# Nine unread matmuls at the start of an attention and expert kernel, and transfers priced by kind in its list schedule

## The chip, the core and the metric

The kernel runs on one core of a Trainium2 chip. The core's engines each work through a queue of their own, in order: TensorE (PE; its weight loads are shown as PEld), VectorE (DVE), ScalarE (ACT), GpSimd (POOL) and SyncE (SP), which here issues nearly all transfers. The metric is the device time of one execution in microseconds, as the median of several runs.

## What is computed

Two batches, eight heads, 768 positions and 64 numbers per head. Attention is masked by a hash: a query sees the keys in the same one of 64 buckets, and the bucket is the signs of six projections. The result goes through two expert stages of dense products, the first with a plain product of two branches, the second with a sigmoid gate.

```python
q_bits = (np.einsum('bhsd,dk->bhsk', q, proj) > 0)      # the same for k
mask = q_bucket[:, :, :, None] == k_bucket[:, :, None, :]
scores = np.where(mask, scale * np.matmul(q, k.transpose(0, 1, 3, 2)), -1000000000.0)
attn = np.exp(scores - max); attn = attn / (sum + 1e-09); x = np.matmul(attn, v)
...
h = ((x @ w1) * (x @ w2)) @ w3;  x = h @ w_out           # 512 -> 1024 -> 1024 -> 512
val = x @ w_val; y = (sigmoid(x @ w_gate) * val) @ w_out # 512 -> 1536 -> 512
```

q, k, v and proj are float32, the weights arrive as 64-bit floats and are decoded on the chip.

## The kernel before

**Precision and tiles.** A float32 operand is split into a high and a low part (both fp32r), and a product is three passes: high by high, high by low, low by high. That is why there are pairs of names: aq and bq, ak and bk, wth and wtl, pt_0 and pt_1.

**Attention, 16 heads.** Per head h, `prep` scales the queries on POOL (L495), casts them to aq (L496), makes the difference bq (L497), each in two halves, and copies parts of them by transfers (L500, L501). The hash of a half is three matmuls with the projection pq (L479) into a bank gps, a sign on ACT (sg, L481), a matmul with a pattern pat (L482) and a comparison on DVE (ft, L504), whose result is moved next to the operands by further transfers (L508 to L510). So the mask is part of the score product itself. `first_head` does the same for head 0 with the work spread over ACT, DVE and POOL (L533 to L546). Per tile g of 128 queries (six per head): scores s (four matmuls, L558 and L561), their maximum sm on DVE (L567), the exponential e with its row sum on ACT (L577), transposes tp on PE (L612), their split into pt_0 on ACT (L615) and pt_1 on DVE (L617), and twelve matmuls av with the split values spv (L630; the split is L466 and L467), for two tiles at a time. Every head's row sums go through `emit_rows`: a sum on POOL (L588), a reciprocal rs, a transfer to a row in DRAM (L591) and a broadcast back into rr (L595). `emit_scale` multiplies the output of a pair of heads in xall by rr on POOL (L602), for t in steps of 2 of 6 chunks, so three instructions of 128x256 per pair; the result is read by the first expert stage only.

**Filler.** Between the tiles the weights come in: `stage_next` issues a load st of 512 KB (L412), and `decode` turns it into float32 with two instructions on ACT (da L428, dr L429), two on POOL (dr L430, da L431) and two on DVE (L432, L437). The product of the last two matrices of the first stage (wacc, L685, from wo and t, split at L673 and L680) and the first part of that stage (L794) run in the same gaps.

**Expert stages.** From about 340 us on it is nearly all `three` (L794), with splits on ACT, POOL and DVE.

**What sets the order.** `order_engines` takes all instructions with their dependencies, buffers and a priority, and runs a list schedule in a model of the chip: `cost` gives each instruction a duration, `step` a delay between engines, a transfer lands by a formula from a single rate, and PE has a clock with two levels. Then 6,000 random changes of priorities are tried, and each that does not lengthen the modelled whole is kept. The order found is imposed on each engine. So a change of one price anywhere in the model can change the order everywhere.

## Time and profile before

| | us |
|---|---|
| three timed runs | 766.24, 766.40, 767.06 |
| median | 766.4 |
| the profiled execution | 769.23 |
| its span, first to last instruction | 767.4 |
| PE busy | 746.2 |
| DVE, ACT, POOL busy | 626.3, 525.3, 431.4 |

The profiled execution's own time is 1.8 us above its span, and 2.8 us above the median. Busy is the time in which an engine works on an instruction, waits left out; matmuls overlap, so a busy PE may still be paced by something. The chain that ended last is made of PE for 81% of the span, of ACT for 7%, DVE 5%, POOL 4%, waits for issue 2% and transfers 2%. Windows are stretches of time counted from the first instruction; the granted clock is the share of TensorE's full clock in a stretch.

### The profile page before, as it was taken

How to read it: one execution, taken by the hardware profiler on the slowest of the kernel's cores; microseconds unless marked ns; L12 is line 12 of the kernel's file. 1: busy time of each engine (PE TensorE's matmuls, PEld its weight loads, DVE VectorE, ACT ScalarE, POOL GpSimd, SP SyncE). 2: the span in 40 equal slices, each digit the busy share in tenths (PEclk: the TensorE clock that was granted, in tenths of full speed). 3: DMA queues.
4: the chain of work that ended last, by engine and by line, in shares of the span. 5: the costliest groups of instructions: out<-in, count | busy, mean ns of one | idle time of the engine just before them, and what ended most of it. 6: DMA issues, size and time to landing. Idle time of an engine off the chain costs nothing.

```text
span 767.4 us, 11480 instructions
## 1 busy us (share of the span) xinstructions
PE 746.2 (97%) x3896; PEld 638.3 (83%) x3896; DVE 626.3 (82%) x970; ACT 525.3 (68%) x986; POOL 431.4 (56%) x475
## 2 busy tenths in 40 slices
PE   5898999999999999999999999999999999999997
PEld 4787889888989889988888888888888888888886
DVE  6996988776899789869999998788789787676743
ACT  7897988877899889777555568865746444442353
POOL 7767787865577574446655544797654433442000
PEclk9999999999999999999999999999999999999999
DMA  9975767533457755200111143432100000000011
GB/s 289 231 175 149 193 175 205 140 100 115 151 148 168 176 141 142 87 12 1 54 40 45 56 164 124 151 125 97 55 0 28 28 1 1 1 0 2 1 55 56
DMA packets 28506, 74.46 MB, mean 97 GB/s; under 512 B 6048, under 2 KB 8352, under 8 KB 28448
## 3 DMA queue, kind: packets, MB, share of 16 engines
q1 hardware_dynamic: 28368, 73.73, 33.1%
q8 instruction: 31, 0.51, 0.3%
q14 instruction: 27, 0.22, 0.1%
q10 hardware_dynamic: 80, 0.00, 0.0%
HBM read 52.82 MB, written 3.19 MB: 73 GB/s over the span
## 4 chain that ended last, share of the span: by engine, by line
PE 81%; ACT 7%; DVE 5%; POOL 4%; issue 2%; DMA 2%; SPq 0%; DVEq 0%; ACTq 0%; POOLq 0%
PE pa L794 18%; PE pb L794 15%; PE m L794 11%; PE av L630 6%; PE wacc L685 5%; PE tp L612 5%; PE p L794 4%; PE npa L794 4%; PE npb L794 4%; PE s L558 3%; PE s L561 3%; ACT e L577 2%; PE y L794 2%; ACT pt L615 2%; PE gps L479 2%
## 5 line engine op out<-in xcount | busy, mean ns | idle before, releaser
L617 DVE TENSOR_TENSOR pt<-tp,pt 128x512 fp32r<-128x512 f32 x144 | 95.0, 683 | 9.0 <-ACT pt L615 8.1
L612 PE MATMUL tp<-idf,e 128*128 128x128 f32 x576 | 100.3, 276 | 1.8 <-DVE xall L643 0.8
L567 DVE TENSOR_REDUCE sm<-s 128x1 f32<-128x768 f32 x96 | 90.2, 948 | 11.3 <-PE s L561 11.0
L577 ACT ACTIVATE e<-s,sm 128x768 f32<-128x768 f32 x96 | 86.9, 906 | 8.1 <-DVE sm L567 7.6
L431 POOL TENSOR_SCALAR da<-da 128x512 f32<-128x512 f32 x76 | 52.4, 689 | 66.1 <-ACT da L428 59.0
L615 ACT ACTIVATE pt<-tp 128x512 fp32r<-128x512 f32 x144 | 82.4, 599 | 8.6 <-PE tp L612 7.2
L612 PEld LDWEIGHTS tp<-idf,e 128*128 128x128 f32 x576 | 72.0, 141 | 11.6 <-DVE xall L643 2.0
L630 PE MATMUL av<-pt,spv 128*128 128x256 f32 x576 | 79.2, 286 | 0.7 <-DVE ft L504 0.3
L630 PEld LDWEIGHTS av<-pt,spv 128*128 128x128 f32 x576 | 73.2, 190 | 3.6 <-DVE pt L617 1.8
L430 POOL TENSOR_SCALAR dr<-st 128x512 bf16<-128x512 f32 x76 | 67.3, 887 | 6.9 <-issue 1.1
L558 PE MATMUL s<-bk,bq 128*128 128x384 f32 x192 | 62.2, 377 | 6.1 <-ACT e L577 5.4
L561 PE MATMUL s<-ak,aq 128*128 128x384 f32 x192 | 60.8, 376 | 0.0
L429 ACT ACTIVATE dr<-st 128x512 int16<-128x512 uint32 x76 | 60.1, 791 | 0.0
L685 PE MATMUL wacc<-wo,t 128*128 128x512 f32 x192 | 59.3, 407 | 0.0
L428 ACT ACTIVATE da<-st 128x512 f32<-128x512 f32 x76 | 51.1, 672 | 12.0 <-DVE xall L437 3.7
L432 DVE TENSOR_SCALAR da<-da 128x512 uint32<-128x512 uint32 x76 | 47.3, 625 | 9.8 <-POOL da L431 9.8
L558 PEld LDWEIGHTS s<-bk,bq 128*128 128x128 f32 x192 | 36.0, 195 | 11.8 <-ACT e L577 7.8
L794 PE MATMUL pa<-xsx,swh 128*128 128x512 f32 x136 | 42.5, 390 | 0.2 <-DVE w2r L957 0.2
L920 POOL TENSOR_TENSOR swl<-w2r,swh 128x512 fp32r<-128x512 f32 x16 | 21.0, 1313 | 31.2 <-ACT swh L367 28.9
L561 PEld LDWEIGHTS s<-ak,aq 128*128 128x128 f32 x192 | 36.6, 195 | 1.8 <-DVE ak L544 0.3
L685 PEld LDWEIGHTS wacc<-wo,t 128*128 128x128 f32 x192 | 34.3, 189 | 4.2 <-ACT t L367 0.2
L794 PE MATMUL m<-wtl,gh 128*128 128x512 f32 x96 | 37.2, 389 | 0.0
(338 smaller groups left out, 2187.3 us busy)
## 6 DMA issues: line engine op xcount, KB each, us to landing
st<-in_moe_w_dram SPq DMA_DIRECT2D x32, 512.0 KB, 5.2
st<-in_moe_w_out_dram SPq DMA_DIRECT2D x20, 512.0 KB, 3.3
st<-in_moe_w_gate_dram SPq DMA_DIRECT2D x12, 512.0 KB, 3.3
st<-in_moe_w_val_dram SPq DMA_DIRECT2D x12, 512.0 KB, 3.2
qk<-in_qk_dram SPq DMA_DIRECT2D x15, 384.0 KB, 4.3
rawv<-in_v_dram SPq DMA_DIRECT2D x16, 192.0 KB, 2.4
rr<-row SPq DMA_DIRECT2D x16, 192.0 KB, 5.0
out_dram<-o SPq DMA_DIRECT2D x12, 256.0 KB, 2.0
```

Source lines behind the costliest of these rows:

```text
L429: act.activation(out=r.bitcast(I16)[:, 0::2], in_=lw, func=AF.Copy, scale=2.0 ** -29)
L430: pool.tensor_scalar(out=r.bitcast(BF16)[:, 1::2], in0=f(hw), scalar1=0.0, scalar2=1.0, op0=ALU.mult, op1=ALU.mult)
L558: pe.matmul(s[:, half, :HS], lhsT=m["bq"][:, qs], rhs=m["bk"][:, ks], start=True, stop=False)
L561: pe.matmul(s[:, half, :HS], lhsT=m["aq"][:, qs], rhs=m["ak"][:, ks], start=False, stop=True)
L567: dve.tensor_reduce(out=b, in_=s[:, :, :HS], op=ALU.max, axis=AX.XY, negate=True)
L577: act.activation(out=e.rearrange("p (a c) -> p a c", a=2), in_=s[:, :, :HS], func=AF.Exp, bias=sm, scale=1.0, accum_out=su_t[h][:, t:t + 1],)
L612: pe.transpose(ps[:, i * P:(i + 1) * P], e_t[g - g % 2 + a][:, c * P:(c + 1) * P], idf)
L615: act.activation(out=dh, in_=src, func=AF.Copy)
L617: dve.tensor_tensor(out=d, in0=src, in1=f(dh), op=ALU.subtract)
L630: pe.matmul(acc[:w.shape[1], :2 * P].rearrange("p (a t) -> p a t", a=2), lhsT=w, rhs=r[:, :, c], start=(c == 0 and i == 0), stop=(c == NT ...
L685: pe.matmul(acc, lhsT=t3[x][:, j], rhs=wo[y][:, j], start=(j == 0 and n == 0), stop=(j == NF1 - 1 and n == 2))
L794: mm = pe.matmul(ps, lhsT=lhs[x], rhs=rhs[y], start=start and n == 0, stop=stop and n == 2)
```

## The change

There are two parts. On the chip, DVE sets a 128x128 piece of xall to zero first, and PE multiplies it by itself five times into a bank named ramp; after each half of head 0's cast and difference PE multiplies them by the projection once more into the same bank, with a priority 150 lower, so that the list schedule places these four where it likes. Nobody reads the bank. The scaling of a pair is written as two instructions of 128x384 in place of three of 128x256. In the model, ACT's price for 256 columns of a bank falls from 405 to 290 ns and DVE's price per column of a small two-operand instruction on a bank from 1.17 to 1.0; a transfer has a delay of 1.7 us in place of 2.9, a rate by kind (250 bytes per ns for 64-bit weights, 205 for what is read from a tile, 340 for the rest, in place of 300 for all) and at least 0.3 us, and lands 3.0 us later where it reads a row in DRAM and 1.0 us later otherwise, in place of 0.9.

```diff
--- before.py
+++ after.py
@@ -95,7 +95,7 @@
             return n / 2.4 * passes + (14 if n == 512 else 16 if passes == 1 else 2 if passes == 2 else 4)
         if e == "Activation":
             if banks:
-                return {768: 878, 512: 478, 256: 405}.get(n, 470)
+                return {768: 878, 512: 478, 256: 290}.get(n, 470)
             return 40 + n + (96 if es == 2 else 0)
         if e == "Pool":
             port[k] = True
@@ -110,7 +110,7 @@
             if two and n >= 512:
                 return 600
             if two:
-                return 85 + n * 1.17 if banks else 60 + n * 1.1
+                return 85 + n * 1.0 if banks else 60 + n * 1.1
             return 589 if banks else 60 + n * 0.55
         return 500
 
@@ -171,6 +171,10 @@
     costs = [cost(k) for k in range(N)]
     left0 = [len(deps[k]) + len(starts[k]) for k in range(N)]
     loads = [type(i).__name__.startswith("InstDMA") for i in ins]
+    wide = [mybir.dt.size(i.outs[0].dtype) == 8 for i in ins]
+    local = [[r[0] for r in map(region, i.ins) if r] for i in ins]
+    rate = [250 if wide[k] else 205 if local[k] else 340 for k in range(N)]
+    slack = [3000 if any(t.startswith("row") for t in local[k]) else 1000 for k in range(N)]
 
     HORIZON, STRIDE = 30000.0, 15000.0
 
@@ -281,8 +285,8 @@
                         free[e] = done = begin + c
                         if loads[k]:
                             n = count(ins[k].outs[0]) * list(ins[k].outs[0].ap)[0][1] * mybir.dt.size(ins[k].outs[0].dtype)
-                            dma = max(now + 2900, dma) + n / 300
-                            done = dma + 900
+                            dma = max(now + 1700, dma) + max(300, n / rate[k])
+                            done = dma + slack[k]
                         tick += 2
                         heapq.heappush(events, (done, tick - 1, "end", k))
                         heapq.heappush(events, (free[e], tick, "free", k))
@@ -518,7 +522,12 @@
         m = mats[0]
         t = [ap_.tile([P, S], F32, tag="e", name=f"qk0{i}", bufs=4) for i in range(2)]
         act.dma_start(out=pq_raw, in_=proj)
+        x = xall[:, 0, 0:P]
+        dve.memset(x, 0.0)
         dve.memset(zb, -2.0 ** -64)
+        ps = psT.tile([P, 512], F32, tag="t", name="ramp")
+        for _ in range(5):
+            pe.matmul(ps[:, :P], lhsT=x, rhs=x, start=True, stop=True)
         act.activation(out=warm, in_=zb, func=AF.Exp)
         for half in range(2):
             hs = slice(half * HS, (half + 1) * HS)
@@ -533,6 +542,10 @@
             act.activation(out=m["aq"][:, hs], in_=t[0][:, hs], func=AF.Copy, scale=scl[:, 0:1])
             dve.scalar_tensor_tensor(out=m["bq"][:, hs], in0=t[0][:, hs], scalar=scl[:, 0:1], in1=f(m["aq"][:, hs]),
                                      op0=ALU.mult, op1=ALU.subtract)
+            tc.cur_priority += 150
+            for x in ("aq", "bq"):
+                pe.matmul(ps[:, :HS], lhsT=pq[0], rhs=m[x][:, hs], start=True, stop=True)
+            tc.cur_priority -= 150
         load_qk(2)
         act_copy(m["bk"][0:D], t[1][0:D])
         dve.tensor_copy(m["bk"][D:P], f(m["bq"][D:P]))
@@ -598,8 +611,8 @@
         b, hh = divmod(h, H)
         x = xall[:, hh // 2, b * S:(b + 1) * S].rearrange("p (c q) -> p c q", c=NT)
         r = rr_t.pop(h // 2).rearrange("p (q c) -> p c q", c=NT)
-        for t in range(0, NT, 2):
-            pool.tensor_tensor(out=x[:, t:t + 2], in0=x[:, t:t + 2], in1=r[:, t:t + 2], op=ALU.mult)
+        for t in range(0, NT, NT // 2):
+            pool.tensor_tensor(out=x[:, t:t + NT // 2], in0=x[:, t:t + NT // 2], in1=r[:, t:t + NT // 2], op=ALU.mult)
 
     def emit_T(g, j):
 
```

The numbers move the order of the whole program. In the next listings a number behind a name is the buffer's, and the lines L of the changed kernel are 4 larger in the decoder, in `prep` and its helpers and 13 larger from `first_head`'s second half on. The first place is POOL around the preparation of head 4 (aq4, bq4) and the scaling of heads 0 and 1 (xall by rr0). Before:

```order
L431 TENSOR_SCALAR da_948<-da_948 128x512
L495 TENSOR_SCALAR qk5_628<-qk5_628 64x384 x2
L430 TENSOR_SCALAR dr_949<-st_705 128x512
L466 CAST spv3_903<-rawv3_532 128x6x64
L467 TENSOR_TENSOR spv3_903<-rawv3_532,spv3_903 128x6x64
L602 TENSOR_TENSOR xall_79<-xall_79,rr0_306 128x256 x3
L496 CAST aq4_776<-qk4_381 128x384
L497 TENSOR_TENSOR bq4_777<-qk4_381,aq4_776 128x384
L496 CAST aq4_776<-qk4_381 128x384
L497 TENSOR_TENSOR bq4_777<-qk4_381,aq4_776 128x384
L588 TENSOR_SCALAR su2_612<-su2_612 128x6
L680 TENSOR_TENSOR wo1_93<-wor3_443,wo0_92 128x512
```

The same place on POOL in the changed kernel:

```order
L693 TENSOR_TENSOR wo1_93<-wor3_454,wo0_92 128x512
L435 TENSOR_SCALAR da_990<-da_990 128x512
L470 CAST spv3_913<-rawv3_543 128x6x64
L471 TENSOR_TENSOR spv3_913<-rawv3_543,spv3_913 128x6x64
L434 TENSOR_SCALAR dr_991<-st_800 128x512
L500 CAST aq4_786<-qk4_392 128x384
L501 TENSOR_TENSOR bq4_787<-qk4_392,aq4_786 128x384
L500 CAST aq4_786<-qk4_392 128x384
L501 TENSOR_TENSOR bq4_787<-qk4_392,aq4_786 128x384
L615 TENSOR_TENSOR xall_79<-xall_79,rr0_317 128x384 x2
L693 TENSOR_TENSOR wo1_93<-wor4_455,wo0_92 128x512
L601 TENSOR_SCALAR su2_623<-su2_623 128x6
```

The scaling went from ahead of head 4's casts to behind them; one wo, one da and one dr came ahead of them. The second place is DVE at the start (pq the projection, pat the pattern made from bits, bq0, bk0 and ak0 operands of head 0, spv0 its split values, sm the maximum). Before:

```order
L1107 TENSOR_TENSOR bits_117<-bits_117 64x128
L1108 TENSOR_SCALAR bits_117<-bits_117 64x128
L1111 TENSOR_SCALAR pat_72<-bits_117 32x64 x2
L1114 CAST pq0_70<-pq_raw_73 64x6 x2
L1115 TENSOR_TENSOR pq1_71<-pq_raw_73,pq0_70 64x6 x2
L534 SCALAR_TENSOR_TENSOR bq0_96<-qk00_100,scl_75,aq0_95 128x384 x2
L538 CAST bk0_98<-bq0_96 64x768
L544 TENSOR_SCALAR ak0_97<-gps_148,thr_74 64x384
L466 CAST spv0_242<-rawv0_111 128x6x64
L544 TENSOR_SCALAR ak0_97<-gps_155,thr_74 64x384
L567 TENSOR_REDUCE sm0_184<-s0_84 128x1
```

DVE at the start of the changed kernel:

```order
L1120 TENSOR_TENSOR bits_124<-bits_124 64x128
L1127 CAST pq0_70<-pq_raw_73 64x6
L1121 TENSOR_SCALAR bits_124<-bits_124 64x128
L1127 CAST pq0_70<-pq_raw_73 64x6
L1128 TENSOR_TENSOR pq1_71<-pq_raw_73,pq0_70 64x6 x2
L1124 TENSOR_SCALAR pat_72<-bits_124 32x64 x2
L543 SCALAR_TENSOR_TENSOR bq0_96<-qk00_100,scl_75,aq0_95 128x384 x2
L551 CAST bk0_98<-bq0_96 64x768
L470 CAST spv0_253<-rawv0_118 128x6x64
L557 TENSOR_SCALAR ak0_97<-gps_159,thr_74 64x384
L557 TENSOR_SCALAR ak0_97<-gps_166,thr_74 64x384
L580 TENSOR_REDUCE sm0_195<-s0_84 128x1
```

The mask of bits and pat went behind the first cast of the projection, which waits for a transfer, and the cast of the values, which waits for another, went ahead of both comparisons ak0. The third place is ACT behind those comparisons, where the first weights are decoded (da, dr) and the first exponentials (e) run. Before:

```order
L546 ACTIVATE aq0_95<-gps_155,nthr_76 64x384
L428 ACTIVATE da_456<-st_448 128x512
L577 ACTIVATE e0_187,su0_186<-s0_84,sm0_184 128x768
L577 ACTIVATE e1_195,su0_186<-s1_85,sm1_193 128x768
L429 ACTIVATE dr_457<-st_448 128x512
L428 ACTIVATE da_466<-st_450 128x512
L481 ACTIVATE sg_225<-gps_221,zb_78 128x384
L429 ACTIVATE dr_467<-st_450 128x512
```

ACT at the same place in the changed kernel:

```order
L559 ACTIVATE aq0_95<-gps_166,nthr_76 64x384
L432 ACTIVATE da_467<-st_459 128x512
L433 ACTIVATE dr_468<-st_459 128x512
L590 ACTIVATE e0_198,su0_197<-s0_84,sm0_195 128x768
L432 ACTIVATE da_477<-st_461 128x512
L590 ACTIVATE e1_206,su0_197<-s1_85,sm1_204 128x768
L433 ACTIVATE dr_478<-st_461 128x512
L485 ACTIVATE sg_236<-gps_232,zb_78 128x384
```

The first weight's dr went ahead of the first exponential, and the second's da ahead of the second.

## Rows read from the trace of the kernel before

**Rows 1.** Page, part 1: busy us, share of the span, instructions, of each engine

```profile
PE 746.2 (97%) x3896; PEld 638.3 (83%) x3896; DVE 626.3 (82%) x970; ACT 525.3 (68%) x986; POOL 431.4 (56%) x475
```

**Rows 2.** Windows of 20 us: busy time by engine, columns as in the first line

```profile
core 0: us, PE busy (x) PEld busy (x) DVE busy (x) ACT busy (x) POOL busy (x), PEclk, DMA share, GB/s
40.00:60.00 20.00, 18.64 (x129) 16.64 (x127) 19.65 (x31) 19.78 (x42) 12.95 (x18) 1.00 0.67 162
60.00:80.00 20.00, 17.44 (x108) 16.15 (x108) 14.17 (x24) 14.55 (x30) 16.39 (x22) 0.91 0.59 153
80.00:100.00 20.00, 19.82 (x132) 17.76 (x132) 19.67 (x31) 19.83 (x41) 15.83 (x19) 1.00 0.61 168
...
360.00:380.00 20.00, 20.00 (x89) 16.19 (x88) 19.82 (x34) 10.49 (x20) 10.41 (x10) 1.00 0.08 26
```

**Rows 3.** Windows of 1 us behind PE's wait near 60 us, same columns

```profile
62.00:63.00 1.00, 0.86 (x3) 0.79 (x4) 0.00 (x0) 0.00 (x0) 0.92 (x2) 0.59 0.00 0
63.00:64.00 1.00, 1.00 (x6) 1.00 (x5) 0.00 (x0) 0.00 (x0) 0.92 (x3) 0.50 0.00 0
64.00:65.00 1.00, 1.00 (x5) 1.00 (x4) 0.00 (x0) 0.54 (x2) 0.89 (x2) 0.50 0.24 58
65.00:66.00 1.00, 1.00 (x6) 1.00 (x5) 0.00 (x0) 1.00 (x3) 0.94 (x1) 0.70 0.98 223
```

**Rows 4.** Timelines of POOL and PE, 55 to 80: start, length, instruction, [idle before <-releaser]

```profile
55.00 1.01 POOL L467 TENSOR_TENSOR spv<-rawv,spv 128x384 fp32r<-128x384 f32 x1
58.53 3.11 POOL L602 TENSOR_TENSOR xall<-xall,rr 128x256 f32<-128x256 f32 x3 [2.52 <-DMA rr<-row]
61.59 0.50 POOL L496 CAST aq<-qk 128x384 fp32r<-128x384 f32 x1
...
74.13 1.30 POOL L680 TENSOR_TENSOR wo<-wor,wo 128x512 fp32r<-128x512 f32 x1 [2.18 <-ACT wo L367]
79.09 0.77 POOL L496 CAST aq<-qk 128x384 fp32r<-128x384 f32 x1 [0.41 <-PE s L561]
...
57.34 1.69 PE L630 MATMUL av<-pt,spv 128*128 128x256 f32 x12
62.14 0.68 PE L479 MATMUL gps<-aq,pq 128*128 128x384 f32 x1 [3.12 <-POOL aq L496]
```

**Rows 5.** The start: four pieces of the chain, then timelines of DVE and ACT

```profile
0.73 2.40 DMA pq_raw<-in_proj_dram
4.58 1.98 PE gps L479 x5
8.54 0.32 PE s L558
36.06 0.18 PE s L561
...
2.31 0.22 DVE L1108 TENSOR_SCALAR bits<-bits 64x128 int32<-64x128 int32 x1
2.57 0.38 DVE L1111 TENSOR_SCALAR pat<-bits 32x64 fp32r<-32x64 int32 x2
8.29 0.55 DVE L466 CAST spv<-rawv 128x384 fp32r<-128x384 f32 x1 [0.64 <-DMA rawv<-in_v_dram]
8.88 0.67 DVE L544 TENSOR_SCALAR ak<-gps,thr 64x384 fp32r<-64x384 f32 x1
10.33 1.82 DVE L567 TENSOR_REDUCE sm<-s 128x1 f32<-128x768 f32 x2 [0.78 <-PE s L561]
...
10.56 0.67 ACT L428 ACTIVATE da<-st 128x512 f32<-128x512 f32 x1 [0.40 <-DMA st<-in_moe_w_dram]
13.09 0.78 ACT L429 ACTIVATE dr<-st 128x512 int16<-128x512 uint32 x1
```

**Rows 6.** Groups of POOL's instructions by form: count, busy us, mean ns

```profile
L430 POOL TENSOR_SCALAR dr<-st 128x512 bf16<-128x512 f32 x76 | 67.3, 887 | 6.9 <-issue 1.1 <-DMA st<-in_moe_w_gate_dram 0.8
L497 POOL TENSOR_TENSOR bq<-qk,aq 128x384 fp32r<-128x384 f32 x30 | 31.9, 1066 | 2.2
```

## Prediction, written before the changed kernel ran

> **What bounds the kernel now.** I read the page first, then the table of 20 us windows, then the two places at which TensorE stands still, on all engines. The page gives TensorE 746.2 us of busy time in a span of 767.4 us [rows 1], but the windows [rows 2] show two different kernels behind that share. From 360 to 380 us, in the first of the two expert stages, PE is busy 20.00 of 20.00 us: there an order can only lose. From 40 to 80 us, in the attention stage, PE is busy 18.64 and 17.44 us per window, while DVE and ACT reach 19.65 and 19.78 us. The window 60 to 80 is odd: PE, DVE and ACT are all low (17.44, 14.17, 14.55 us) and the granted clock is 0.91. Something holds all three.
>
> Rows 3 and 4 show what. GpSimd (POOL) stands in front of the scaling of the first two heads' output (L602) for 2.52 us, until the broadcast of the row sums has landed; then three multiplications take 3.11 us; only then comes the cast aq of head 4, at 61.59. PE ended its last work at 57.34 + 1.69 = 59.0 and waits for that cast, 3.12 us, up to 62.14 [rows 4]. After that wait the granted clock falls: 0.59, 0.50, 0.50 and 0.70 in the four microseconds from 62 to 66, for most of them the lower of the two levels (1.2 GHz) [rows 3]. This is the longest wait of PE behind its first matmul.
>
> **The change, part by part.** The profiled execution took 769.2 us, its span 767.4; the three timed runs have a median of 766.4. I make the sum as a difference on the profiled one and carry the difference over to the median, 2.8 us lower.
>
> *The scaling behind head 4.* In the new order POOL issues both casts and both differences of head 4 first and the scaling after them. One product wo, one da and one dr stand there in its place, taken from behind the casts. The wo and the da come before the split of the values, and this split waits for other things in any case; only the dr lies between the split's end (55.00 + 1.01 = 56.0 [rows 4]) and the cast. It takes 0.89 us in the mean [rows 6], so the cast can start near 57, not at 61.59. PE reaches the hash matmuls at 59.0. Since the new order keeps more of them in a row, it needs the last difference about 1 us later; this one is there at 57 + 2 x (0.50 + 1.07) = 60.1 [rows 4, 6]. I take 0.4 us of wait for that, against 3.12 us that go. With the hole goes the low clock: from 62 to 66 the clock lost 0.41 + 0.50 + 0.50 + 0.30 = 1.71 us of work [rows 3]. Together -3.12 - 1.71 + 0.4 = -4.4. Late next are DVE and ACT: they are nearly full from 40 to 60 and from 80 to 100 (DVE 19.65 and 19.67, ACT 19.78 and 19.83), but from 60 to 80 they have 5.8 and 5.4 us to spare [rows 2], because of this hole. So they can follow by 4.4 us. Bounds: 0 (another wait of the same size takes its place) and -4.8.
>
> *The same scaling, in the next round.* Behind head 4's casts it lies ahead of head 5's. From the cast of head 4 to that of head 5 POOL issues the same kinds of rows as often as before, plus the scaling, now as two instructions of 128x384. For one of these I take the 1.07 us of the difference L497, of the same size and also with two operands [rows 6]: 2.1 us. In before, POOL had two waits in this round, 2.18 us for ACT's wo and 0.41 us ahead of head 5's cast at 79.09 [rows 4]: 2.6 us of room, of which 0.5 is left. I take +0.5 us on PE for what does not fit; bounds 0 and +2.1, if the present waits all stay.
>
> *The first 26 us.* Five matmuls of zeros and four on head 0's operands are added on PE, ahead of and between the hash matmuls. PE does nothing before 3.73 and waits between these, so they cost nothing where they stand, as long as each ends before the operand of the next one is there. What they act on is the clock: a score matmul on the chain took 0.32 us at 8.54 and 0.18 us at 36.06, so the clock was at its lower level in the first, though no row of the clock says so; five hash matmuls are 1.98 us of the chain [rows 5]. But the chain does not get this time, because of what the new order does on DVE. There the mask L1108 (0.22 us) and the two rows of pat L1111 (0.38 us), which ran while the small projection was on its way (0.73 + 2.40 = 3.13), now stand behind the first cast of it: +0.6 us for bq and the hash matmuls. And the split of head 0's values, which waits for its transfer until 8.29 and takes 0.55 us, now stands ahead of both comparisons ak (0.67 us each), not between them [rows 5]: ak is whole at 8.29 + 0.55 + 2 x 0.67 = 10.2, not at 8.88 + 0.67 = 9.55. So a faster PE hides behind a transfer, and the first maximum is late by 0.65 us. On ACT the first weight's da and dr stand ahead of the first exponential, the second's da ahead of the second: 0.67 and 0.78 us of decoding [rows 5] that used to come after both. The exponentials come some 1 and 1.5 us later; but ACT is nearly full from here to 60, so the decoding is paid earlier and not twice, and ACT loses only the later end of the two comparisons. I take +0.6 us for all of it; bounds 0 and +1.5 (the whole delay of the second exponential).
>
> *The rest.* Scaling with two instructions and not three saves POOL some time, beside other work: nothing. The order of the expert stages is redrawn too; PE has no wait to lose there, and DVE has only 0.18 us free in the window 360 to 380 [rows 2]: 0, bounds 0 and +1.5. In the attention stage behind 100 us small waits may come and go: 0, bounds -2 and +2.
>
> Sum: -4.4 + 0.5 + 0.6 = **-3.3 us**: 769.2 - 3.3 = 765.9 for a profiled execution, 766.4 - 3.3 = **763.1** for the median.
>
> **The rivals.**
> (a) *POOL becomes the late one at head 5.* If POOL's waits of this round stay, head 5's cast is 2.1 us late; PE waits as long, and the clock falls as at 62 to 66, 1.7 us. Then -3.3 - 0.5 + 2.1 + 1.7 = 0: 766.4. For it: the room of 0.5 us. Against: POOL's waits may be there because ACT and DVE stood still in the hole; these go with it.
> (b) *Slower: the same at more heads.* The new order puts the scaling behind the first or both casts also for heads 6, 8 and 10. If POOL is late by the 2.1 us of the scaling in two rounds, with the clock each time, that is 2 x 3.8 = 7.6 us in place of the 0.5: -3.3 - 0.5 + 7.6 = +3.8, 770.2. It decides where POOL's idle time in a round is below 2.1 us. For it: POOL is busy 16.39 us in the window 60 to 80, the most of these rows. Against: 15.83 us from 80 to 100 leave 4 us [rows 2].
> (c) *The zeros lift the clock and this counts in full.* The low-clock matmuls on the chain, from 4.58 to the first maximum at 10.33, are less than 1.98 + 9 x 0.32 = 4.9 us; at 0.18 in place of 0.32 some 2.2 us less. If the chain gets that, because the values' transfer lands sooner or does not bind, the start is -2.2 in place of +0.6: 760.3. Against it stands the transfer that lands at 8.29, ahead of DVE's two comparisons. The Trainium skill (TensorE: Matmul & The Clock Gate, Part 1) says that a throttled clock is the default and that activity releases it; by that rule the zeros would bring the clock forward, and the trace agrees as far as the 0.32 and 0.18 us go.
> (d) *The added matmuls do not bring the clock forward*: PE idles between them. Since nothing was credited to the clock in the start, this too gives 763.1.
>
> **How the numbers follow.** Forecast, (d) in it, 0.50; (a) 0.20; (b) 0.18; (c) 0.12. The forecast's own range, from its bounds, is 760.5 to 764.8. For 8 in 10 the range must take in (a) whole, half of (b) and half of (c): **759.0 to 768.8**. About 0.2% (1.5 us) is what a measurement of this kernel can tell from no change. Faster by more than that: 0.50 + 0.12 = 0.62; same: 0.20; slower: 0.18.
>
> **What would show it.** PE's wait for head 4's cast near 59 us is gone, with no lower clock at 62 to 66, and PE is busy above 19 us from 60 to 80. Head 5's cast starts by 75 us. The first maximum starts at 10.7 to 11.0, not at 10.33, and the exponentials 1 to 1.5 us later than before. PE matmuls before 9 us are 0.18 us apart if the clock came early. I am wrong if POOL's scaling waits again in front of a cast that PE needs, if PE has waits over 1 us in the expert stages, or if the start is late by more than 1.5 us at the second head's first scores.

## The result and the profile after

The changed kernel takes 775.66 us (median of 4 runs, 773.66 to 777.12), the kernel before 766.73 (4 runs): a ratio of 1.0115, 95% interval 1.0093 to 1.0138. It is slower by 8.9 us, where 3.3 us less were forecast; the time lies 6.9 us above the upper end of the range. The profiled execution, 777.12 us with a span of 775.3, is the longest of the four. One execution of the kernel before, 774.62 us, fell in a slower state and is left out of all comparisons.

| | before | after |
|---|---|---|
| median, us | 766.73 | 775.66 |
| profiled execution / its span, us | 769.23 / 767.4 | 777.12 / 775.3 |
| PE busy 20 to 40, and its clock | 17.97, 0.91 | 14.61, 0.91 |
| PE busy 60 to 80, and its clock | 17.44, 0.91 | 19.96, 1.00 |
| PE busy 80 to 100 | 19.82 | 18.10 |
| PE busy 360 to 380 | 20.00 | 18.46 |
| first row maximum starts, us | 10.33 | 11.98 |

Page, part 1, and windows of 20 us of the changed kernel (columns as in [rows 2]; they answer to [rows 1, 2]):

```profile
PE 753.5 (97%) x3910; PEld 640.9 (83%) x3910; DVE 639.1 (82%) x971; ACT 527.3 (68%) x986; POOL 430.3 (55%) x467
...
20.00:40.00 20.00, 14.61 (x90) 13.09 (x88) 17.80 (x25) 15.93 (x33) 12.79 (x17) 0.91 0.72 203
60.00:80.00 20.00, 19.96 (x131) 17.65 (x131) 19.92 (x31) 19.08 (x40) 18.42 (x23) 1.00 0.64 174
80.00:100.00 20.00, 18.10 (x122) 15.84 (x121) 18.82 (x28) 17.78 (x36) 13.20 (x17) 1.00 0.71 179
360.00:380.00 20.00, 18.46 (x81) 14.87 (x81) 19.67 (x31) 8.95 (x17) 9.37 (x8) 1.00 0.00 0
```

The window that I wanted filled is full: from 60 to 80 us PE, DVE and ACT are all above 19. The others lost. At head 4 (timeline of POOL, then of PE; answers to [rows 4]) the casts now come ahead of the scaling, and PE's hash matmuls have no wait in front of them:

```profile
61.32 1.11 POOL L434 TENSOR_SCALAR dr<-st 128x512 bf16<-128x512 f32 x1
62.34 0.51 POOL L500 CAST aq<-qk 128x384 fp32r<-128x384 f32 x1
...
65.45 2.63 POOL L615 TENSOR_TENSOR xall<-xall,rr 128x384 f32<-128x384 f32 x2
...
64.57 0.41 PE L483 MATMUL gps<-aq,pq 128*128 128x384 f32 x1
```

At the start (POOL, PE, DVE, ACT; answers to [rows 5]) POOL prepares half of head 1, for which it waits 0.61 us, before it writes bq of head 0. PE has issued its last unread matmul (ramp) at 8.51 and stands 1.26 us in front of the first scores:

```profile
7.16 0.51 POOL L499 TENSOR_SCALAR qk<-qk 64x384 f32<-64x384 f32 x1 [0.61 <-DMA qk<-in_qk_dram]
9.40 0.83 POOL L554 TENSOR_SCALAR bq<-qk 64x768 fp32r<-64x768 f32 x1
...
8.51 0.52 PE L547 MATMUL ramp<-bq,pq 128*128 128x384 f32 x1
10.29 1.01 PE L571 MATMUL s<-bk,bq 128*128 128x384 f32 x2 [1.26 <-POOL bq L554]
...
11.98 0.96 DVE L580 TENSOR_REDUCE sm<-s 128x1 f32<-128x768 f32 x1 [2.25 <-PE s L574]
...
12.97 0.90 ACT L590 ACTIVATE e<-s,sm 128x768 f32<-128x768 f32 x1 [1.25 <-DVE sm L580]
```

**Where the time went.** PE does the same work in all these kernels, the nine matmuls aside. So I give each matmul its usual spacing at full clock (0.174 us for 384 columns, 0.095 for 128, 0.119 for 256, 0.228 for 512), add these up in the order of issue without the nine, and note when each trace reaches a sum. The runs other than before and after are told below; here they have the first part of their names only. before, before_2 and e12_scale_wo (one place moved, near 60 us) have the order before; after, e3_thin, e5_zeros (one row moved at the start) and e10_late (three rows moved, behind 200 us) have the changed one.

```
work us   before before_2      e12       e6       e8       e9       f1       f5    after       e3       e5      e10
     12     27.7     26.7     28.8     29.6     30.7     28.1     29.4     31.3     32.0     32.1     31.8     31.9
     35     55.2     54.2     56.1     57.1     57.6     56.4     56.6     57.6     60.5     59.4     59.5     59.4
     45     70.8     66.1     67.0     71.9     68.5     67.5     68.9     69.6     71.3     70.6     70.7     70.2
     70     98.5     93.8     95.5     99.6     97.1     97.5     98.1     98.8    101.3     98.5     98.6     98.1
    240    280.5    274.9    277.9    283.6    282.1    281.3    281.3    283.3    286.7    285.0    283.6    282.5
    300    343.2    337.7    340.6    346.3    344.6    344.3    344.4    347.1    349.6    347.9    346.5    345.4
    350    393.2    387.7    390.6    396.4    394.6    394.8    394.4    399.0    402.1    400.4    399.0    399.7
    715    757.0    751.5    754.5    760.2    757.9    758.9    757.5    762.4    765.3    763.6    762.1    762.8
```

From before to after: +5.3 us up to work 35, -4.8 from there to 45 (head 4), +5.9 from 45 to 300, +2.5 from 300 to 350 (first expert stage), -0.6 behind it. That is +8.3. But each column is one execution. Against before_2 the same stretches give +6.3, -1.1, +6.7, +2.5 and -0.6: most of the gain at head 4 belongs to the execution before. The losses are there in every trace of the changed order: 3 to 5 us up to work 12 (31.8 to 32.1 against 26.7 to 28.8), 2 to 5 us from 70 to 240 (184.4 to 186.5 against 181.1 to 182.4), 2.5 us from 300 to 350 (in e10_late 4.3).

### The profile page after: what moved, and what is told of

It is laid out like the page before. It is cut to its first block, busy times and chain, and to the rows that moved or that the text cites. A ratio compares the mean times of both kernels' runs of the same rounds, so it can differ in the third digit from the quotient of the medians.

```text
span 775.3 us, 11509 instructions
## 1 busy us (share of the span) xinstructions
PE 753.5 (97%) x3910; PEld 640.9 (83%) x3910; DVE 639.1 (82%) x971; ACT 527.3 (68%) x986; POOL 430.3 (55%) x467
## 4 chain that ended last, share of the span: by engine, by line
PE 77%; POOL 6%; DVE 5%; ACT 5%; DMA 4%; issue 3%; SPq 1%; POOLq 0%; ACTq 0%
PE pa L807 18%; PE pb L807 15%; PE m L807 11%; PE av L643 6%; PE tp L625 5%; PE npb L807 4%; PE npa L807 4%; PE p L807 3%; PE wacc L698 3%; PE s L571 3%; PE s L574 2%; PE y L807 2%; DMA qk<-in_qk_dram 2%; ACT e L590 2%; POOL bq L501 1%
## 5 line engine op out<-in xcount | busy, mean ns | idle before, releaser
L625 PE MATMUL tp<-idf,e 128*128 128x128 f32 x576 | 95.8, 275 | 2.7 <-DVE ft L508 1.2
L625 PEld LDWEIGHTS tp<-idf,e 128*128 128x128 f32 x576 | 70.4, 140 | 13.3 <-DVE xall L656 2.8
L434 POOL TENSOR_SCALAR dr<-st 128x512 bf16<-128x512 f32 x76 | 68.5, 904 | 8.0 <-DVE w2r L441 1.9
L571 PE MATMUL s<-bk,bq 128*128 128x384 f32 x192 | 60.2, 374 | 6.4 <-ACT e L590 5.0
L436 DVE TENSOR_SCALAR da<-da 128x512 uint32<-128x512 uint32 x76 | 57.8, 763 | 8.6 <-POOL da L435 8.4
L807 PE MATMUL m<-wth,gh 128*128 128x512 f32 x96 | 36.9, 389 | 0.0
```

What stands on the lines that cost most here:

```text
L434: pool.tensor_scalar(out=r.bitcast(BF16)[:, 1::2], in0=f(hw), scalar1=0.0, scalar2=1.0, op0=ALU.mult, op1=ALU.mult)
L571: pe.matmul(s[:, half, :HS], lhsT=m["bq"][:, qs], rhs=m["bk"][:, ks], start=True, stop=False)
L625: pe.transpose(ps[:, i * P:(i + 1) * P], e_t[g - g % 2 + a][:, c * P:(c + 1) * P], idf)
L807: mm = pe.matmul(ps, lhsT=lhs[x], rhs=rhs[y], start=start and n == 0, stop=stop and n == 2)
```

## Experiments

The experiments ran in five groups, each beside its own runs of the kernel before, whose median lay between 766.2 and 767.9; so ratios are compared. Their intervals are 0.2 to 0.5% to either side, 1.3 to 3.9 us; the changed kernel's own is 1.0093 to 1.0138. In most runs the order that the planner found is kept and single rows are moved in it: move(engine, row, ahead or behind another row). The edits are cut to the lines that matter.

### Was the wait at head 4 there to be won?

**e4_scale**, the step of the prediction alone, in the order before (the first three rows of xall are the scaling of heads 0 and 1):

```diff
+    last = rows("Pool", "bq4_777")[-1]
+    for k in reversed(rows("Pool", "xall_79")[:3]):
+        move("Pool", k, behind=last)
```

> The kernel before with one move: the three rows of GpSimd that scale heads 0 and 1 (58.53 to 61.6 us) go behind the four rows that cast head 4's operands. Nothing else is changed. Theory (the step of the prediction on head 4 is right by itself, 3.1 us of wait and 1.7 us of low clock, less 0.4): 4.4 us less than 766.7, so 761.5 to 763.0, a ratio of 0.993 to 0.995. Rival (the gain at head 4 is taken back by a later round, as it is in the changed kernel): 765 to 767, a ratio above 0.997.

Measured: 766.80 us, ratio 0.9997 (0.9978 to 1.0017). Its profiled execution (765.27 us) is 4.0 us faster than that of before; the medians don't differ. So one of the two profiles may show an uncommon execution, and I ran the kernel before once more.

**before_2**, no edit.

> The kernel before, unchanged, profiled once more: its first profiled execution took 769.2 us where its other runs lie at 766.2 to 766.8, and moving the scaling alone won 3.9 us between two profiled executions but nothing between the medians. Theory 1 (TensorE's wait of 3.12 us at head 4 depends on when a transfer lands and is shorter in the common execution): the wait ahead of about 62 us is under 1 us here. Theory 2 (the wait is always there, and the difference lies in the clock or elsewhere): the wait is 2.5 to 3.2 us again.

Measured: 763.69 us, span 761.9. The same instructions at head 4 (POOL, then PE; compare [rows 4]):

```profile
54.95 2.52 POOL L602 TENSOR_TENSOR xall<-xall,rr 128x256 f32<-128x256 f32 x3
57.42 0.50 POOL L496 CAST aq<-qk 128x384 fp32r<-128x384 f32 x1
...
59.12 0.44 PE L479 MATMUL gps<-bq,pq 128*128 128x384 f32 x1 [0.20 <-POOL bq L497]
```

There is no wait for the broadcast, and PE waits 0.20 us, not 3.12. The view of the tile rr in this stretch gives the transfer itself, its issue on SP's queue (ns, start) and the time to its landing, first in before, then in before_2:

```profile
L595 SPq DMA_DIRECT2D rr<-row x1: 865/865/865, 50.7 to 50.7; - x1
...
DMA to landing us min/median/max: 7.7/7.7/7.7
```

```profile
L595 SPq DMA_DIRECT2D rr<-row x1: 595/595/595, 50.3 to 50.3; - x1
...
DMA to landing us min/median/max: 3.8/3.8/3.8
```

Issued 0.4 us apart, it landed after 7.7 us in one execution and after 3.8 in the other. In runs told below, with few rows of this order moved, it took 3.4 (e12_scale_wo), 5.1 (e4_scale), 6.8 (g1_best) and 6.9 us (e6_nine). Theory 1 holds: the wait that carried my forecast belongs to some executions only. It is not rare, though. In the third execution in which the scaling stands ahead of the casts, that of e6_nine, PE waits 2.37 us:

```profile
63.30 0.69 PE L481 MATMUL gps<-aq,pq 128*128 128x384 f32 x1 [2.37 <-POOL aq L498]
```

**e12_scale_wo**: as e4_scale, but behind the sum su and two products wo as well, since in e4_scale PE waited for wo twice.

```diff
+    o = order["Pool"]; x = o.index(rows("Pool", "bq4_777")[-1])
+    last = [k for k in rows("Pool", "wo1_93") if o.index(k) > x][1]
+    for k in reversed(rows("Pool", "xall_79")[:3]):
+        move("Pool", k, behind=last)
```

> The kernel before with the three rows that scale heads 0 and 1 behind the four casts of head 4, the sums su and the two wo rows behind them (in e4_scale they stood ahead of su and wo, and TensorE waited 0.34 + 0.29 us for wo). Theory (the wait of 3.12 us at head 4 falls away in every execution, and wo is no longer late): 1 to 2.5 us less than the kernel before in the median, a ratio of 0.9965 to 0.999. Rival (rows behind it are late by as much, as in e4_scale): 0.999 to 1.001.

Measured: 766.54 us, 0.9986 (0.9964 to 1.0009). The interval takes in no change. So the step at head 4 is worth between 2.8 us less and 0.7 us more in the median, not 4.4 less. It may take away long executions: of 99 executions of the kernel before, in all groups, 17 took more than 769.4 us, and of the 34 with the scaling moved (e4_scale, e12_scale_wo, g1_best) none did. I saw this afterwards and made no run for it.

### What do the nine unread matmuls cost?

**e2_bq0**, in the order after: head 0's bq goes back ahead of head 1's first half.

```diff
+ move("Pool", rows("Pool", "bq0_96")[0], ahead=rows("Pool", "qk1_116")[0])
```

> The changed kernel with one row of GpSimd moved: the first head's bq (63 rows, 0.83 us) goes ahead of the first half of head 1's preparation, where it stands in the kernel before; in the changed kernel it waits there for head 1's qk, which lands at 7.08 us. Theory (this row alone makes the first scores late: TensorE's idle 1.26 us ahead of 10.29 us): the first scores at about 8.5 to 9.0 us, the first exp 1.2 to 1.7 us earlier, 1 to 1.7 us less than 775.7 in the end: 774.0 to 774.7. Rival (ScalarE's da and dr, ahead of the exps, or the wait of 2.69 us for ScalarE's exp at 22.95 us take it up): under 0.5 us, 775.2 to 776.

Measured: 776.36 us, 1.0120 (1.0086 to 1.0154): nothing won. POOL's timeline says why:

```profile
9.18 0.83 POOL L554 TENSOR_SCALAR bq<-qk 64x768 fp32r<-64x768 f32 x1 [2.59 <-PE ramp L547]
```

The row stands at the head of its queue and waits 2.59 us for PE's unread matmul. That matmul reads bq over all 128 partitions, and POOL is about to overwrite 64 of them.

**e3_thin**: the nine matmuls with 4 columns, the order kept.

```diff
-            pe.matmul(ps[:, :P], lhsT=x, rhs=x, start=True, stop=True)
+            pe.matmul(ps[:, :4], lhsT=x, rhs=x[:, 0:4], start=True, stop=True)
...
-                pe.matmul(ps[:, :HS], lhsT=pq[0], rhs=m[x][:, hs], start=True, stop=True)
+                pe.matmul(ps[:, :4], lhsT=pq[0], rhs=m[x][:, half * HS:half * HS + 4], start=True, stop=True)
```

> The changed kernel with the order of every engine as it is, but the nine unread matmuls 4 columns wide in place of 128 and 384. What they compute is read by nothing in either. Theory (the nine matmuls neither lift the clock nor delay a read matmul, since the scores wait for GpSimd's bq until 10.29 us): within 1 us of 775.7, the clock at full speed at the same place, about 17.9 us. Rival 1 (they do work on the clock): the clock rises later, 1 to 3 us more, 777 to 779. Rival 2 (they stand in the way): the first scores earlier and 0.5 to 1.5 us less.

Measured: 773.69 us, 1.0095 (1.0064 to 1.0127), not to be told from the changed kernel. The width is not what costs. In this trace POOL's bq starts at 9.54, right behind the rows of head 1; in after these rows end at 9.32 and bq starts at 9.40. So in the changed order the readers' hold, which e2_bq0 puts at 9.18, is hidden behind head 1's rows.

**e5_zeros**: the move of e2_bq0, and the four matmuls read the zeros instead of the operands.

```diff
-            for x in ("aq", "bq"):
-                pe.matmul(ps[:, :HS], lhsT=pq[0], rhs=m[x][:, hs], start=True, stop=True)
+            for _ in range(2):
+                pe.matmul(ps[:, :P], lhsT=x, rhs=x, start=True, stop=True)
```

> The changed kernel with GpSimd's bq row of the first head ahead of head 1's first half (as in the run e2_bq0), and with the four unread matmuls on the first head's operands made matmuls on the zeros. Theory (in e2_bq0 the bq row still started at 9.18 us, since it overwrites rows that the last unread matmul reads until 9.0 us; without that reader it starts at 6.6 us): bq at 6.6 to 7.4 us, the first scores at 8.5 to 9.0 us in place of 10.07 to 10.29, the first maximum at 10.2 to 10.9 us, and 0.7 to 1.5 us less than 776.4 in the end. Rival (bq waits for another reader or for the transfer): bq stays at about 9 us and the time at 776.

Measured: 773.57 us, 1.0060 (1.0027 to 1.0094). POOL's bq, and the first maximum on DVE:

```profile
7.23 0.84 POOL L554 TENSOR_SCALAR bq<-qk 64x768 fp32r<-64x768 f32 x1 [1.25 <-PE gps L483]
...
10.89 1.82 DVE L580 TENSOR_REDUCE sm<-s 128x1 f32<-128x768 f32 x2 [0.73 <-PE s L574]
```

The reader was what held bq in e2_bq0: here bq is 1.95 us earlier. The maximum gains less: 10.89, in e2_bq0 11.07, in e10_late, which starts with the same rows as after, 11.46 (after: 11.98, at a lower clock, see the last section). It now waits for both comparisons ak behind the values' transfer, as I had reckoned (10.7 to 11.0). And by work 12 nothing is left: 31.8 us, in e10_late 31.9, in after 32.0. The time is below that of the changed kernel, 4.2 us going by the ratios and 2.1 by the times, but the traces don't show that the earlier bq is the reason.

**e6_nine**: the fill of zeros and the nine matmuls, put into the order before, nothing else moved (five ahead of the first gps, one behind it, three ahead of the first s).

```diff
+    for k in at[1:6]:
+        o.insert(o.index(gps[0]), k)
...
+    o.insert(o.index(gps[0]) + 1, at[6])
+    for k in at[7:]:
+        o.insert(o.index(s), k)
```

> The kernel before with the fill of zeros and the nine unread matmuls put into its own order, everything else as it is: five at the head of TensorE's queue, one behind the first gps matmul, three ahead of the first scores. Theory (the last of them holds GpSimd's bq row, and so the first scores): bq at 8.2 to 8.8 us in place of 6.64, the first scores at 9.2 to 9.7 us in place of 7.53, the first exp 1.3 to 2 us later, and 0.5 to 1.5 us more than 766.2 in the end. Rival 1 (the matmuls lift the clock early, and that pays for it): 765 to 766. Rival 2 (waits that stand behind it anyway take the delay up): within 0.3 us of 766.2.

Measured: 770.02 us (10 runs), 1.0038 (1.0013 to 1.0064): +2.9 us, by the interval 1.0 to 4.9, where I expected 0.5 to 1.5, with the mechanism that I expected (PE, then POOL, then PE):

```profile
7.62 0.52 PE L546 MATMUL ramp<-bq,pq 128*128 128x384 f32 x1
...
8.23 0.84 POOL L553 TENSOR_SCALAR bq<-qk 64x768 fp32r<-64x768 f32 x1 [1.78 <-PE ramp L546]
...
9.12 0.44 PE L570 MATMUL s<-bk,bq 128*128 128x384 f32 x1 [0.98 <-POOL bq L553]
```

The first scores come at 9.12, in before_2 at 7.59; the third exponential at 21.20, in before_2 at 19.56. By work 12 the table above shows 29.6 us against 27.7, 26.7 and 28.8 (e12_scale_wo), and by 35 it is still 1.9, 2.9 and 1.0 behind: the late start is not made good. What stands behind 35 in this trace is not the matmuls' alone, since it has the wait of 2.37 us at head 4.

### Held rows of VectorE, and the late waits

Two rows of VectorE are several times as long as usual in the trace of after, while GpSimd issues row after row (DVE, POOL, PE around 24 us; then DVE and PE around 91 us):

```profile
23.88 2.86 DVE L436 TENSOR_SCALAR da<-da 128x512 uint32<-128x512 uint32 x1
26.66 0.94 DVE L580 TENSOR_REDUCE sm<-s 128x1 f32<-128x768 f32 x1
...
23.24 1.09 POOL L499 TENSOR_SCALAR qk<-qk 64x384 f32<-64x384 f32 x2
24.30 1.00 POOL L471 TENSOR_TENSOR spv<-rawv,spv 128x384 fp32r<-128x384 f32 x1
25.27 0.77 POOL L434 TENSOR_SCALAR dr<-st 128x512 bf16<-128x512 f32 x1
25.96 0.50 POOL L500 CAST aq<-qk 128x384 fp32r<-128x384 f32 x1
26.54 1.06 POOL L501 TENSOR_TENSOR bq<-qk,aq 128x384 fp32r<-128x384 f32 x1
...
28.95 0.41 PE L483 MATMUL gps<-aq,pq 128*128 128x384 f32 x1 [1.58 <-DVE pt L630]
...
90.76 2.73 DVE L441 CUSTOM_DVE_ANT_0 w3f<-da,dr 128x1024 uint16<-128x1024 uint16 x1
...
94.00 1.69 PE L643 MATMUL av<-pt,spv 128*128 128x256 f32 x12 [1.62 <-DVE xall L656]
```

In the four other executions that leave both rows in place (e2_bq0, e3_thin, e5_zeros, e10_late) da takes 2.43 to 2.88 us again, but w3f 0.68, as here in e10_late:

```profile
89.64 0.68 DVE L441 CUSTOM_DVE_ANT_0 w3f<-da,dr 128x1024 uint16<-128x1024 uint16 x1
```

So the wait at 94 us belongs to one execution, like that at head 4.

**e1_port**: both go behind the row maximum that followed them (o[b - 2] is the w3f row).

```diff
+    move("DVE", rows("DVE", "da_649")[0], behind=rows("DVE", "sm4_278")[0])
+    o, b = order["DVE"], order["DVE"].index(rows("DVE", "sm26_1246")[0])
...
+    move("DVE", o[b - 2], behind=o[b])
```

> The changed kernel with two rows of VectorE moved one place each: the AND on da (23.88 us, 2.86 us long in the trace of the changed kernel) behind the row maximum that followed it, and the merge into w3f (90.76 us, 2.73 us long) behind the xall add and the row maximum that followed it. Theory (VectorE's row is held while GpSimd runs row after row, and what stands behind it on VectorE makes TensorE wait 1.58 + 0.70 us at 29 us and 1.62 us at 94 us): these waits go, 2 to 4 us less than the changed kernel's 775.7, so 771.7 to 773.7, a ratio of 1.006 to 1.009 to the kernel before. Rival (VectorE is full there, so the next row is late by as much): within 1 us of 775.7, a ratio of 1.010 to 1.013.

Measured: 773.58 us, 1.0085 (1.0056 to 1.0114). In its new place da is short again:

```profile
26.09 0.42 DVE L436 TENSOR_SCALAR da<-da 128x512 uint32<-128x512 uint32 x1
```

The time is 2.1 us below after's, the lower end of the theory, but the intervals overlap, and the traces give the moves next to nothing: e1_port reaches work 70, behind both of them, at 98.0 us, e10_late, which has moved neither, at 98.1, e3_thin at 98.5. Only after's execution is later, at 101.3.

**e10_late**: three more rows, behind 200 us.

```diff
+ move("Activation", rows("Activation", "pt0_60_2964")[0], ahead=rows("Activation", "da_3069")[0])
+ move("DVE", rows("DVE", "da_4313")[0], behind=rows("DVE", "ft14_3575")[1])
+ move("DVE", rows("DVE", "p0_4649")[0], ahead=rows("DVE", "xsx2_1_1_4734")[-1])
```

> The changed kernel with three rows moved behind 200 us: ScalarE's first copy of pt at 227.6 us goes ahead of da and dr (226.4 us); VectorE's ft at 282.9 us goes ahead of the AND on da that is held 1.48 us at 281.5 us; VectorE's p at 371.5 us goes ahead of the two xsx rows (369.2 us, the second one held). Theory (each is what TensorE waits for: 1.09 us at 229.0, 1.22 us at 283.6 and 1.54 us at 372.9): 0.6 + 1.2 + 1.4 = 3.2 us less than the changed kernel, a ratio of 1.006 to 1.009 to the kernel before where the changed kernel has 1.0115. Rival (the next row on VectorE is late by as much): less than 1 us.

Measured: 773.15 us, 1.0084 (1.0058 to 1.0110); again the interval overlaps that of after. The trace does not put the 2.5 us between the two times down to the moves: e10_late is 3.2 us ahead of after at work 70, where nothing has been moved yet, and 2.4 at 350, behind all three. One of the three moves worked: PE's wait of 1.22 us for ft is gone. The wait at 229 us shrank from 1.09 to 0.95 only, and the one in the expert stage was handed to the next row, gl, which stands behind the same xsx rows. Behind the longer wait there the clock falls, to 0.57 from 370 to 374 us. PE in after, then in e10_late, and that window (columns as in [rows 2]):

```profile
283.60 0.66 PE L625 MATMUL tp<-idf,e 128*128 128x128 f32 x4 [1.22 <-DVE ft L508]
...
372.85 0.96 PE L807 MATMUL y<-gh,wh 128*128 128x512 f32 x3 [1.54 <-ACT gh L371]
```

```profile
225.71 1.69 PE L643 MATMUL av<-pt,spv 128*128 128x256 f32 x12 [0.95 <-DVE pt L630]
...
370.07 0.51 PE L807 MATMUL y<-gl,wh 128*128 128x512 f32 x1 [1.80 <-DVE gl L770]
...
370.00:374.00 4.00, 3.93 (x10) 3.12 (x11) 3.77 (x8) 0.11 (x1) 0.00 (x0) 0.57 0.00 0
```

**e11_all**: all of these moves, and the third maximum and its exponential earlier (the two new moves are shown).

```diff
+ move("DVE", rows("DVE", "sm2_212")[0], ahead=rows("DVE", "da_467")[0])
+ move("Activation", rows("Activation", "e2_214")[0], ahead=rows("Activation", "t30_0_485")[0])
```

> The changed kernel with all the moves so far (e1_port, e5_zeros with its bq row, e10_late) and one more at the start: the third row maximum, whose scores are there at 14.3 us, goes ahead of VectorE's two da rows (from 15.8 us), and its exp on ScalarE ahead of the wait for w3f (18.2 us). Theory (the losses are separate waits and add up: 2.1 for the held rows, 2.2 for the start, 3.2 for the late rows, 2 to 3 for the third maximum): 9.5 to 10.5 us less than 775.7, so 765 to 766.5, level with the kernel before or just below. Rival (each move only hands the wait on): above 769.

Measured: 773.50 us, 1.0087 (1.0061 to 1.0114). The rival holds: nothing adds up. With e3_thin, which moves no row, e1_port, e5_zeros, e10_late and e11_all lie between 773.15 and 773.69 us, whatever was moved. At the start the wait was handed on, to PE's wait of 1.71 us for ft at 20.25 us.

**g1_best** tried the same two moves in the order before, on top of e12_scale_wo.

```diff
+ move("DVE", rows("DVE", "sm2_201")[0], ahead=rows("DVE", "da_456")[0])
+ move("Activation", rows("Activation", "e2_203")[0], ahead=rows("Activation", "t30_0_474")[0])
```

> The kernel before with the move of e12_scale_wo and one more at the start: the third row maximum (17.8 us in the trace, its scores are there at about 14 us while VectorE idles for 2.5 us) goes ahead of VectorE's first da row, and its exp on ScalarE (19.6 us) ahead of the copy that waits for w3f (16.4 us). Theory (TensorE's wait of 1.9 to 2.2 us for that exp at 20.6 us shrinks by 1 to 1.9 us, on top of what e12_scale_wo won): 0.9945 to 0.998, 762.5 to 765.5. Rival (as in e11_all, the wait is handed on to the next row, ft or pt): 0.998 to 1.0005.

Measured: 767.31 us, 0.9995 (0.9977 to 1.0013), nothing won. PE, in before_2 and in g1_best:

```profile
20.61 0.44 PE L558 MATMUL s<-bk,bq 128*128 128x384 f32 x1 [1.93 <-ACT e L577]
```

```profile
20.47 0.88 PE L612 MATMUL tp<-idf,e 128*128 128x128 f32 x6 [1.24 <-DVE ft L504]
24.22 0.44 PE L558 MATMUL s<-bk,bq 128*128 128x384 f32 x1 [1.65 <-ACT e L577]
```

**f3_hold** and **f4_hold_model** put the hold into the planner (f3 with the numbers before, f4 with those of the change), with 64 ns between two rows of GpSimd as well, and draw a new order:

```diff
-            ("PE", "PE"): 0, ("Activation", "Activation"): 0, ("Pool", "Pool"): 0,
+            ("PE", "PE"): 0, ("Activation", "Activation"): 0, ("Pool", "Pool"): 64,
...
+                        if port[k] and e == "DVE" and lock["Pool"] > now:
+                            free[e] = 1e18
+                            tick += 1
+                            heapq.heappush(events, (lock["Pool"], tick, "grant", k))
+                            continue
```

> The kernel before with the planner changed so that a VectorE row that meets a running GpSimd row starts only when GpSimd pauses, where it started at the end of that row. Theory (c), the hold is what plan and chip disagree on: the order drawn is better than the one before, 758 to 764. Rival (b), any new draw scatters: 766 to 773.

> The run e8_model (only the change's numbers for the planner, 770.4 us) with the hold of f3_hold in the planner as well. Theory (c): 3 us or more below e8_model, 762 to 767. Rival (b): 767 to 774.

Measured: 784.38 us, 1.0232 (1.0189 to 1.0275), and 785.76, 1.0250 (1.0204 to 1.0296), both 15 us and more above what they start from, far more than a new draw costs below. The theory falls: a plan that holds every such row is much worse, which fits a hold that is the exception. The two edits of the planner were not run apart. In f3_hold the first two windows are emptier than in before_2 (PE 9.96 and 16.37 us against 12.40 and 18.03), and DVE is emptier with PE:

```profile
0.00:20.00 20.00, 9.96 (x26) 7.61 (x27) 11.11 (x31) 12.93 (x22) 13.67 (x27) 1.00 0.90 299
20.00:40.00 20.00, 16.37 (x84) 14.51 (x83) 15.57 (x25) 15.82 (x32) 14.39 (x19) 0.83 0.63 157
```

```profile
0.00:20.00 20.00, 12.40 (x44) 9.92 (x44) 12.38 (x35) 14.66 (x26) 14.97 (x27) 1.00 0.92 289
20.00:40.00 20.00, 18.03 (x124) 16.23 (x125) 19.51 (x32) 18.75 (x39) 15.98 (x20) 1.00 0.85 224
```

### The draw of the order

The planner's order comes from a random search, and any edit of its numbers or of the instructions draws a new one. **e8_model** has only the change's numbers, **e9_rest** only the nine matmuls and the halves; **f1_seed2** and **f2_seed3** are the kernel before with another seed, **f5_seed2_after** is the changed kernel with another seed.

```diff
-            return {768: 878, 512: 478, 256: 405}.get(n, 470)
+            return {768: 878, 512: 478, 256: 290}.get(n, 470)
...
-                            dma = max(now + 2900, dma) + n / 300
-                            done = dma + 900
+                            dma = max(now + 1700, dma) + max(300, n / rate[k])
+                            done = dma + slack[k]
```

```diff
-    rng = random.Random(1)
+    rng = random.Random(2)
```

> The kernel before with only the planner's numbers of the change (transfers by kind, the two prices); the nine matmuls and the scaling in halves are left out. The planner draws a new order of all engines. Theory 1 (the loss is the new draw, which knows nothing of VectorE's rows held by GpSimd, and not the matmuls): 770 to 776. Theory 2 (the loss comes with the nine matmuls and the halves): 763 to 767.

> The changed kernel without the planner's new numbers: the nine unread matmuls and the scaling in halves, under the costs of the kernel before. The planner draws a new order here too. Theory (the loss is the sum of two parts that each lose 2 to 4 us, the new numbers 2.8 us by the run e8_model, the nine matmuls 2.9 us by the run e6_nine): 768 to 772, a ratio of 1.002 to 1.007. Rival (the new numbers and the matmuls only lose together): 765 to 767.

> The kernel before with another seed of the planner's random search (2 in place of 1), nothing else changed. Theory (b), an order drawn anew from the same numbers scatters by some us and the order before is one of the better ones: 768 to 774. Theory (a), the numbers decide and the draw hardly matters: 765.5 to 768.

> The kernel before with seed 3 of the planner's random search in place of 1, nothing else changed. Theory (the order before is one of the better draws): 768 to 773 again, a ratio of 1.002 to 1.008. Rival (seed 2 was a bad one, and draws lie on both sides): 762 to 767.5.

> The changed kernel with another seed of the planner's random search (2 in place of 1), nothing else changed. Theory (b), the draw scatters: 767 to 774, some us away from 775.7. Theory (a), the new numbers and the matmuls decide: 774 to 777 again.

| run | us | ratio, 95% interval |
|---|---|---|
| e8_model | 770.41 | 1.0037 (1.0018 to 1.0055) |
| e9_rest | 770.64 | 1.0049 (1.0031 to 1.0066) |
| f1_seed2 | 769.31 | 1.0035 (1.0007 to 1.0063) |
| f2_seed3 | 769.03 | 1.0023 (1.0000 to 1.0046) |
| f5_seed2_after | 774.33 | 1.0103 (1.0053 to 1.0154) |

Two other seeds of the same kernel lose 0.23 and 0.35%, 1.8 and 2.7 us; the interval of the former reaches down to no change. So the order before is the best of three draws of its own planner. The new numbers alone lose 0.37%, which is about what a new draw loses without them; the medians don't show them to be better or worse. The table of traces hints at the start: by work 12 the orders drawn with the new numbers stand at 30.7 (e8_model, without the matmuls), 31.3 and 32.0 us, those drawn anew with the old ones at 28.1 (e9_rest, with the matmuls) and 29.4 (f1_seed2). The changed kernel is no unlucky draw either: another seed gives 1.0103, though with a wide interval.

## Why the prediction was wrong

**The scaling behind head 4 (-4.4): the mechanism was right, the size was not there.** In after's trace the wait and the low clock behind it are gone, and 4.8 us with them. But I priced the wait at what one execution showed. It was 3.12 us there, 0.20 in before_2 and 2.37 in e6_nine, with transfers of 7.7, 3.8 and 6.9 us; against before_2 the changed kernel gains 1.1 us in this stretch, not 4.8. I had noted that the execution lies 2.8 us above the median and carried the difference over in full; it should have made me doubt the largest wait in it. In e4_scale and e12_scale_wo the step is worth -0.03 and -0.14%, with intervals from -0.36 to +0.17%; -4.4 us would have been -0.57%. Why so little is left in the median, when two of three executions have the wait, stays open.

**The next round (+0.5): nothing to correct.** PE has no wait at head 5; POOL is busy 18.42 us from 60 to 80. Head 5's cast starts at 81.11, not by 75, but PE does not wait for it.

**The first 26 us (+0.6, bounds 0 and +1.5): the step that failed in kind.** Two parts of it failed. The first: I wrote that the nine matmuls cost nothing where they stand as long as each ends before the next operand is there. I looked at what they wait for and not at who waits for them: the four on head 0's operands are readers, and POOL's bq has to wait for the last of them. e6_nine prices that at 2.9 us by itself, in the order before. In after POOL's bq also stands behind half of head 1, whose operand lands at 7.16, and this alone keeps it until 9.40; I had not listed that row among those that moved. The second: I wrote that on ACT the early decoding "is paid earlier and not twice". The third exponential, for which PE waits 2.69 us up to 22.95 in after, is late by 2.3 us against before_2 (after, then before_2):

```profile
21.90 0.90 ACT L590 ACTIVATE e<-s,sm 128x768 f32<-128x768 f32 x1
```

```profile
19.56 0.91 ACT L577 ACTIVATE e<-s,sm 128x768 f32<-128x768 f32 x1
```

It is as late where the first scores are repaired (e5_zeros, 22.10). So the start loses 3 to 5 us up to work 12 where I had +0.6, and most of that loss is the order's, not the readers'; which row makes it is not shown. What I reckoned for DVE came out once nothing held bq: the first maximum at 10.89 in e5_zeros. In after it came at 11.98. Whether the matmuls brought the clock forward, rivals (c) and (d), is told in the last section: they may have, but the chain did not get the time.

**The rest (0; bounds -2 and +2 behind 100 us, 0 and +1.5 in the expert stages): too narrow.** Between work 45 and 300 after lost 5.9 us, in the first expert stage 2.5. In the trace these are waits of 0.5 to 1.6 us, among them those behind the two held rows; e1_port and e10_late remove some singly, e11_all more of them together, and none of the three can be told from the changed kernel or from one another. I treated a newly drawn order as neutral and put it at 0 without a reason. Two seeds say that a new draw from this planner costs 1.8 to 2.7 us against the order that was there.

**The slower rival (b) had another mechanism.** It put the loss on scaling that waits at more heads. In after no scaling waits for its transfer. That the whole redrawn order could be worse, at many places by a little, was in none of the four cases, and so neither in the range. The forecast's own range was also added up wrongly: its bounds give 759.6 to 773.5, not 760.5 to 764.8. The measured time lies above even that.

**What adds up, and what stays open.** A draw (1.8 to 2.8 us, with e8_model's) and the nine matmuls (2.9 us) make 4.7 to 5.7 of the 8.9 us; that is arithmetic between separate runs, each uncertain by 1.4 us or more. e9_rest holds a draw and the matmuls together and loses only 3.8. So some 3 to 5 us come only where the new numbers and the matmuls meet, and the cause of these is not shown. With rows moved at seven places e11_all still stands at 1.0087. The changed order with the nine matmuls left out, and other seeds of e8_model and e9_rest, were not run; they would part the matmuls, the numbers and the draw. Whether the numbers make the planner too hopeful at the start, where after is 4 to 5 us late by 32 us and e8_model 3 to 4, or whether these are two draws on the bad side, is not settled. No version beat the kernel before by more than its interval; e12_scale_wo comes nearest.

## What to carry to other kernels

A wait that ends with a transfer is worth what it costs in the common execution: profile the kernel twice before crediting its removal, above all when the profiled execution lies above the median. Work whose result nobody reads still reads: look for the next writer of each operand on every engine. Before a move in an order is credited with a gain, see in the traces whether the time is won behind the moved row or was there ahead of it. And where a change makes a search draw the whole order anew, try other seeds of the kernel before first; their scatter, here 0.23 and 0.35% for two seeds, both on the slow side of the order that was there, belongs into the sum as a cost.
